# A decode layer's last weight columns spread unevenly over the DMA engines, and the last projection's tail cut anew

## The chip, the cores and the metric

One core of one Trainium2 chip runs the kernel. The metric is the device time of one execution in microseconds. Weights, cache and vectors lie in the chip's memory (DRAM) and are brought into the core's on-chip memory of 128 partitions by 16 DMA engines, which the issuing queues of SyncE (SP) and ScalarE (ACT) share. TensorE (PE) multiplies, VectorE (DVE), ScalarE and GpSimd (POOL) do the rest.

## The reference

One token of each of two sequences goes through a layer norm and then through attention over a cache and a gated linear unit in parallel; both results are added to x.

```python
W = min(4096, max(256, Sk // 4))                     # 4096 keys of 32768
xn = layernorm(x)                                    # [2, 1, 512]
q = (xn @ wq).reshape(B, 1, 32, 128)                 # 32 heads, 8 key heads
o = softmax(q @ k[-W:].T * 128 ** -0.5) @ v[-W:]
h = (xn @ W_gate) * (xn @ W_gate > 0) * (xn @ W_up)  # [2, 1, 1792]
out = x + o.reshape(B, 1, 4096) @ wo + h @ W_down
```

All is float32. The bytes are the 16 tiles of keys and values (4 MB each), wq and wo (8 MB each) and w_gate, w_up and w_down (3.5 MB each): 95 MB for two rows of x, so the work per byte is small.

## The kernel before, in words

**The ring.** All large operands go through one on-chip buffer, `ring` (L71), of four places of 8192 columns on 128 partitions. `place` hands the places out in turn: wq takes places 0 and 1, w_gate 2, w_up 3, then each tile of keys or values takes one, and at the end w_down and the two halves of wo. A place is loaded again when its last reader is done, which the issuing queue waits for. The first four tiles of the cache are two of keys (places 0 and 1, wq's) and two of values (place 2, w_gate's, and place 3, w_up's).

**Queues.** x (in three pieces, L121), all keys and values (L106), w_down (L95) and wo (L431) are issued by SyncE; wq, w_gate and w_up (L81) by ScalarE at the start, one behind the other, each as 128 rows, one to a partition. A transfer of 128 rows is divided among the 16 DMA engines, eight rows each.

**Order of the work.** The order on each engine is the order of the program. After the layer norm (L187 to L204) PE transposes xn (L208), VectorE copies it out 16 times over (xnT, L210), and PE multiplies with wq (L220). Then follow the products with w_gate and w_up (L257): x is the stationary operand of 32 columns, and the 1792 columns of the weight are cut into four quarters of 448 that go to four quarters of the PE array, so that four products run side by side. Row p of the on-chip tile holds the four rows 4p to 4p+3 of the weight, so there are four steps `kc`. VectorE forms h (hh, L266) and turns it (L270). Only behind that stand the first keys.

Then come four groups of one cache half and one sequence. In each, VectorE transposes two tiles of keys in halves (kT, L285), PE forms the scores (L291), a softmax follows (L306 to L327), and PE multiplies with two tiles of values (L348).

**The end.** y is summed in two ways. `slot` (L409) multiplies 128 rows of a weight by the stationary operand in one of four quarters of the PE array, taken in turn, over all 512 columns, into y4. Once `EARLY` of these are through, VectorE copies y4 to `ys` (L440), and four products with `fold` sum the quarters into y_ps. The rows of wo that are left go straight into y_ps as four products of 128 columns each (`quarters`, L416). ScalarE copies y_ps out (L444) and issues the store (L445). In words: w_down has 14 steps, each half of wo 16 rows (`j`); 8 steps of w_down go first, then the first half of wo, which comes in two transfers of eight rows, then 6 steps of w_down, then rows 0 to 7 of the second half as slots and rows 8 to 15 as quarters. The second half comes in four transfers (rows 0 to 7, 8 to 12, 13 and 14, 15).

Of the kernel before, what the change touches and what calls it, by code (L numbers as in the profile page):

```python
# [9 lines left out]
F32 = mybir.dt.float32  # L10
# [10 lines left out]
def kernel(  # L21
# [12 lines left out]
    nc = tc.nc  # L34
    P = 128
    B, _, D = x.shape
# [3 lines left out]
    F = w_gate.shape[1]  # L40
    W = min(4096, max(256, SK // 4))
    KC = D // P
# [3 lines left out]
    Q = 4  # L46
    C = 4
    R = HKV // C
# [14 lines left out]
    work = ctx.enter_context(tc.tile_pool(name="work", bufs=2))  # L63
    ps_kt = ctx.enter_context(tc.tile_pool(name="ps_kt", bufs=2, space=PSUM))
    ps_s = ctx.enter_context(tc.tile_pool(name="ps_s", bufs=1, space=PSUM))
    ps_1 = ctx.enter_context(tc.tile_pool(name="ps_1", bufs=1, space=PSUM))
# [7 lines left out]
    def place(cols):  # L74
        lo = taken[0] % RING * RW
        taken[0] += -(-cols // RW)
        return ring[:, lo:lo + cols]

    def load_rows(w):
        t = place(KC * w.shape[1])  # L80
        nc.scalar.dma_start(t, w.rearrange("(p k) f -> p (k f)", p=P))  # L81
        return t.rearrange("p (k f) -> p k f", k=KC)
# [5 lines left out]

    FM = F // P
    MQ = P * FM // Q  # L90
    assert P * FM == F

    def load_down():
# [16 lines left out]
    NJ = HQ * DH // (R * P)  # L110
# [3 lines left out]
    def wo_rows(r, j0, j1):  # L114
        rows = NJ * P
        return wo[r * rows:(r + 1) * rows, :].rearrange("(p j) e -> p j e", p=P)[:, j0:j1, :]
# [3 lines left out]
    for c0, c1 in ((0, 256), (256, 384), (384, 512)):  # L120
        nc.sync.dma_start(x2[:, c0:c1], x[:, 0, c0:c1])  # L121
    wqt = load_rows(wq)

    ident = const.tile([P, P], F32, name="ident")
    make_identity(nc, ident)
# [12 lines left out]
    oT = const.tile([P, R, NJ, B, 16], F32, name="oT")  # L138
# [64 lines left out]
    xn = work.tile([B, D], F32, name="xn", tag="qs")  # L203
    nc.vector.tensor_scalar(xn, xc, rs2, None, op0=ALU.mult)  # L204

    xt_ps = ps_1.tile([P, KC, B], F32, name="xt_ps", tag="misc")
    for kc in range(KC):
        nc.tensor.transpose(xt_ps[:, kc], xn.rearrange("r (p k) -> r k p", k=KC)[:, kc], ident[0:B, 0:B])  # L208
    xnT = work.tile([P, KC, 32], F32, name="xnT", tag="on", bufs=1)
    nc.vector.tensor_copy(  # L210
        xnT.rearrange("p k (b s) -> p k b s", b=B), xt_ps[:, :, :, None].to_broadcast([P, KC, B, 16])
    )


# [1 line left out]
    for kc in range(KC):  # L216
        for r in range(R):
            for c in range(C):
# [2 lines left out]
                    q_ps[r][32 * c:32 * c + 32, :], xnT[:, kc, :], wqt[:, kc, n * 512:(n + 1) * 512],  # L221
                    start=(kc == 0), stop=(kc == KC - 1),
                )
    gw = load_rows(w_gate)
    uw = load_rows(w_up)
    qT = work.tile([P, R, B, C, REP], F32, name="qT", tag="qT", bufs=1)
    for r in range(R):
        qs = work.tile([P, 512], F32, name=f"qs{r}", tag="qs")
# [13 lines left out]
    for pb in range(PB):  # L242
        rows = slice(L * pb, L * pb + L)
        for a in range(NP):
            lo = 2 * a * 16 + pb * REP
# [5 lines left out]

    g_ps = ps_kt.tile([P, MQ], F32, name="g_ps", tag="kt")
    u_ps = ps_kt.tile([P, MQ], F32, name="u_ps", tag="kt")
    for h, dst, wt in ((0, g_ps, gw), (1, u_ps, uw)):
        for kc in range(KC):
            for c in range(Q):
                nc.tensor.matmul(  # L257
                    dst[32 * c:32 * c + 32, :], xnT[:, kc, :], wt[:, kc, c * MQ:(c + 1) * MQ],
                    start=(kc == 0), stop=(kc == KC - 1),
                )  # L260
    gs = work.tile([P, MQ], F32, name="gs", tag="qs")
    nc.scalar.copy(gs, g_ps)
    gr = work.tile([P, MQ], F32, name="gr", tag="qs")
    nc.vector.scalar_tensor_tensor(gr, gs, 0.0, gs, op0=ALU.is_gt, op1=ALU.mult)
# [135 lines left out]
    nc.tensor.matmul(y_ps, xsel.rearrange("p e b s -> p (e b s)"), xr, start=True, stop=False)  # L400

    y4 = ps_kt.tile([P, D], F32, name="y4", tag="kt")
    cuts = {0: (0, NJ // 2, NJ), 1: (0, 8, 13, 15, NJ)}
    EARLY = FM + NJ + cuts[1][1]
    done = [0]

    def slot(lhsT, w):
        t, i = done[0] % Q, done[0]
        nc.tensor.matmul(  # L409
            y4[32 * t:32 * t + 32, :], lhsT.rearrange("p b s -> p (b s)"), w, start=(i < Q), stop=(i >= EARLY - Q)  # L410
        )
        done[0] += 1

    def quarters(lhsT, w, stop):
        for e in range(Q):
            nc.tensor.matmul(  # L416
                y_ps[32 * e:32 * e + 17, :], lhsT, w[:, e * P:(e + 1) * P], start=False, stop=stop
            )
# [4 lines left out]
    def down(k0, k1):  # L423
        for k in range(k0, k1):
            slot(hT[:, k], dw[:, k])

    down(0, 2 * Q)
    for r in range(R):
        wt = place(NJ * D).rearrange("p (j e) -> p j e", j=NJ)
        for j0, j1 in zip(cuts[r], cuts[r][1:]):  # L430
            nc.sync.dma_start(wt[:, j0:j1], wo_rows(r, j0, j1))  # L431
        if r == R - 1:
            down(2 * Q, FM)
        for j in range(NJ):
            if (r, j) < (1, cuts[1][1]):
                slot(oT[:, r, j], wt[:, j])
                continue
            if j == cuts[1][1]:
                ys = work.tile([P, D], F32, name="ys", tag="qs")
                nc.vector.tensor_copy(ys, y4)  # L440
                quarters(fold[:, 0:17], ys, False)
            quarters(oT[:, r, j].rearrange("p b s -> p (b s)")[:, 0:17], wt[:, j], (r, j) == (R - 1, NJ - 1))
    yo = work.tile([P, P], F32, name="yo", tag="yo", bufs=1)
    nc.scalar.copy(yo, y_ps)  # L444
    nc.scalar.dma_start(out[:, 0, :].rearrange("b (e f) -> e b f", e=Q), yo[0:P:16, :])  # L445
# [28 lines left out]
```

## Time and profile before

| | |
|---|---|
| median of 3 runs | 229.83 us (229.8 to 229.96) |
| the profiled execution | 229.9 us |
| its span, first to last instruction | 228.0 us |
| PE, DVE, ACT, POOL busy | 67%, 44%, 3%, 3% of the span |
| bytes moved | 95.03 MB, 417 GB/s over the span |
| ScalarE's queue and SyncE's queue | 15.74 MB and 79.17 MB |

Times in the views are microseconds from the span's start. A line of the timeline gives start, length, engine, source line, operation, what is written from what, how many, and in brackets how long the engine was idle before it and what ended that. A line of the windows gives a stretch, the busy time of each engine in it, the granted clock of PE, the mean busy share of the 16 DMA engines and GB/s; a DMA row counts in the stretch where it starts. In the list of issues the last figure is the time from issue to landing. In the chain of waits a line gives start, length and what the time went to.

### The profile page before, as it was taken

The numbers are of one execution on the slowest core, as the hardware profiler recorded it, in microseconds if no ns is written. First come the engines' busy times: TensorE is split into PE (matmuls) and PEld (weight loads), VectorE is DVE, ScalarE is ACT, GpSimd is POOL, SyncE is SP. The second block draws the span as 40 slices with busy tenths as digits, with TensorE's granted clock in tenths as the row PEclk, the third lists the DMA queues.
The fourth block names the chain that finished last, engine by engine and source line by source line (L and its number), as shares of the span: only waits on it lengthen the run. The fifth ranks groups of instructions, "written<-read, shape, count | busy, mean of one in ns | idle before, by whom it ended". The sixth has DMA issues, their size and how long they took to land.

```text
span 228.0 us, 2005 instructions
## 1 busy us (share of the span) xinstructions
PE 153.7 (67%) x870; PEld 45.0 (20%) x870; DVE 100.0 (44%) x89; ACT 6.8 (3%) x16; POOL 6.1 (3%) x21
## 2 busy tenths in 40 slices
PE   0010977036397668998668968858899885889764
PEld 0000223011121132331122212213131221222212
DVE  2040013003999223999421499922169972213000
ACT  0010012000000010000010000010000001000000
POOL 8100000000000000000000000000000000000000
PEclk9999999857589979999979999985799999599999
DMA  9898999999999999999999999999999999999991
GB/s 368 368 437 379 458 434 439 426 448 408 431 454 420 414 457 420 408 460 435 414 431 454 408 425 457 402 431 454 420 420 445 443 414 431 433 410 425 428 401 59
DMA packets 3792, 95.03 MB, mean 417 GB/s; under 512 B 434, under 2 KB 456, under 8 KB 712
## 3 DMA queue, kind: packets, MB, share of 16 engines
q1 hardware_dynamic: 3324, 79.17, 80.9%
q10 hardware_dynamic: 460, 15.74, 16.3%
q8 instruction: 7, 0.11, 0.2%
q14 instruction: 1, 0.01, 0.0%
HBM read 94.90 MB, written 0.00 MB: 416 GB/s over the span
## 4 chain that ended last, share of the span: by engine, by line
DMA 67%; DVE 14%; PE 9%; issue 8%; ACTq 1%; ACT 0%; DVEq 0%
DMA ring<-in_A_k_cache_dram 37%; DMA ring<-in_B_W_up_dram 21%; DVE kT L285 12%; DMA ring<-in_A_wo_dram 8%; PE u_ps L257 2%; PE s L291 2%; PE o L348 2%; PE pp L333 1%; PE y_ps L416 1%; PE y L409 1%; DVE pt L335 1%; DVE hh L266 0%; ACTq L81 0%; DVE ys L440 0%; DVE m L306 0%
## 5 line engine op out<-in xcount | busy, mean ns | idle before, releaser
L285 DVE STREAM_TRANSPOSE kT<-ring 128x4096 f32<-128x4096 f32 x16 | 70.0, 4417 | 7.0 <-DMA ring<-in_A_k_cache_dram 7.0
L291 PE MATMUL s<-kT,qz 128*32 128x512 f32 x256 | 58.3, 616 | 13.9 <-DVE kT L285 13.9
L348 PE MATMUL o<-ring,pt 128*32 128x512 f32 x256 | 33.0, 661 | 4.5 <-DVE rl L339 4.5
L291 PEld LDWEIGHTS s<-kT,qz 128*32 128x32 f32 x256 | 13.6, 109 | 57.7 <-issue 38.8
L333 PE MATMUL pp<-p,perm 128*128 128x512 f32 x16 | 13.4, 990 | 4.5 <-ACT p L327 4.5
L357 DVE TENSOR_TENSOR on<-o,mask 128x512 f32<-128x512 f32 x8 | 5.4, 676 | 23.6 <-PE o L348 23.6
L348 PEld LDWEIGHTS o<-ring,pt 128*32 128x32 f32 x256 | 8.1, 120 | 25.5 <-issue 20.7
L220 PE MATMUL q_ps<-ring,xnT 128*32 128x512 f32 x64 | 8.8, 710 | 5.9 <-DMA ring<-in_A_wq_dram 5.9
L257 PE MATMUL u_ps<-ring,xnT 128*32 128x448 f32 x32 | 5.3, 828 | 11.0 <-DMA ring<-in_B_W_up_dram 11.0
L335 DVE STREAM_TRANSPOSE pt<-pp 128x1024 f32<-128x1024 f32 x4 | 5.0, 1250 | 17.2 <-PE pp L333 17.2
L208 PE MATMUL xt_ps<-ident,xn 2*128 2x2 f32 x4 | 0.6, 252 | 16.4 <-DVE xn L204 16.4
L363 PE MATMUL oa<-on,picks 128*128 128x512 f32 x16 | 9.0, 645 | 3.7 <-DVE on L357 3.7
L409 PE MATMUL y<-ring,oT 128*32 128x512 f32 x48 | 5.7, 596 | 2.9 <-DMA ring<-in_A_wo_dram 2.9
L306 DVE TENSOR_REDUCE m<-s 128x1 f32<-128x512 f32 x4 | 2.8, 692 | 11.1 <-PE s L291 11.1
L266 DVE TENSOR_TENSOR hh<-gr,u_ps 128x448 f32<-128x448 f32 x1 | 0.9, 908 | 15.0 <-PE u_ps L257 15.0
L235 DVE COPY qT<-qt 128x32 f32<-128x32 f32 x2 | 0.4, 192 | 15.8 <-PE qt L232 15.8
L327 ACT ACTIVATE p<-s,nm 128x512 f32<-128x512 f32 x4 | 2.7, 687 | 150.3 <-DVE nm L321 150.3
L299 PE MATMUL idle<-pt,ident 128*128 128x512 f32 x12 | 6.0, 618 | 0.0
L333 PEld LDWEIGHTS pp<-p,perm 128*128 128x128 f32 x16 | 3.8, 261 | 8.2 <-issue 4.6
L440 DVE COPY ys<-y 128x512 f32<-128x512 f32 x1 | 0.7, 692 | 10.7 <-PE y L409 10.7
L187 DVE BATCH_NORM_STATS2 stats<-x 2x6 f32<-2x512 f32 x1 | 0.7, 682 | 10.6 <-DMA x<-in_A_x_dram 10.6
L220 PEld LDWEIGHTS q_ps<-ring,xnT 128*32 128x32 f32 x64 | 2.4, 128 | 11.4 <-issue 11.4
(72 smaller groups left out, 59.8 us busy)
## 6 DMA issues: line engine op xcount, KB each, us to landing
ring<-in_A_k_cache_dram SPq DMA_DIRECT2D x8, 4096.0 KB, 28.5
ring<-in_A_v_cache_dram SPq DMA_DIRECT2D x8, 4096.0 KB, 24.2
ring<-in_A_wo_dram SPq DMA_DIRECT2D x3, 2048.0 KB, 28.5
ring<-in_B_W_gate_dram ACTq DMA_DIRECT2D x1, 3584.0 KB, 30.1
ring<-in_B_W_up_dram ACTq DMA_DIRECT2D x1, 3584.0 KB
ring<-in_B_W_down_dram SPq DMA_DIRECT2D x1, 3584.0 KB, 29.0
ring<-in_A_wo_dram SPq DMA_DIRECT2D x1, 1280.0 KB
ring<-in_A_wo_dram SPq DMA_DIRECT2D x1, 512.0 KB, 21.4
```

Of the source, the lines that this page charges most:

```text
L220: nc.tensor.matmul(q_ps[r][32 * c:32 * c + 32, :], xnT[:, kc, :], wqt[:, kc, n * 512:(n + 1) * 512], start=(kc == 0), stop=(kc == KC - 1),)
L257: nc.tensor.matmul(dst[32 * c:32 * c + 32, :], xnT[:, kc, :], wt[:, kc, c * MQ:(c + 1) * MQ], start=(kc == 0), stop=(kc == KC - 1),)
L285: nc.vector.transpose(kt.rearrange("p j c k h -> p (j c k h)"), kt_in[:, JH * s1 * DH:JH * (s1 + 1) * DH])
L291: nc.tensor.matmul(ss[g][lo:lo + 32, :], qz[:, g, cb, h, 16 * a:16 * a + 32], kt[:, :, cb, :, h], start=(a == 0 and cb == 0), stop=(a == N ...
L299: nc.tensor.matmul(idle, ident, pts[g][:, 2 * n:2 * n + 2].rearrange("p n j k -> p (n j k)"), start=True, stop=True)
L306: nc.vector.tensor_reduce(out=m, in_=ss[g], op=ALU.max, axis=AX.X)
L333: nc.tensor.matmul(pp[:, h], perm[:, h], p, start=True, stop=True)
L335: nc.vector.transpose(pts[g].rearrange("p n j k -> p j n k"), pp.rearrange("p h y -> p y h"))
L348: nc.tensor.matmul(o[32 * q:32 * q + 32, :], pts[g][:, a * S1 + s1, j:j + 4, :].rearrange("p u k -> p (u k)"), v[:, lo:lo + 512], start=(s ...
L357: nc.vector.tensor_tensor(ons[a], os[a].rearrange("p (u d) -> p u d", u=4), mask[:, :, None].to_broadcast([P, 4, P]), op=ALU.mult)
L363: nc.tensor.matmul(oa[g].rearrange("p u e j -> p u (e j)"), picks[:, a].rearrange("p h a i e -> p (h a i e)"), ons[a], start=(a == 0), sto ...
L409: nc.tensor.matmul(y4[32 * t:32 * t + 32, :], lhsT.rearrange("p b s -> p (b s)"), w, start=(i < Q), stop=(i >= EARLY - Q))
```

## The change

**w_up.** Its place is loaded with all but the last 320 columns of the last of the four rows on each partition (`UC`: 6848 of 7168 columns). Those 128 pieces of 320 columns (1280 bytes) go elsewhere: into four strips of 320 columns behind, which are set to zero first. `SMALL` lists four transfers: two of 20 pieces over five engines into strip 0 (four pieces each), and two of 36 pieces over three engines into strips 1 to 3 (twelve each); a fifth brings the last 16 pieces over 16 engines. All five stand behind w_up's main part on ScalarE's queue. A piece's partition is then no longer that of its row of x, so the last of the four parts of xn is laid out again for each strip (`xe`, by GpSimd), transposed by PE into four further columns of xnT, and multiplied with the strips in four further products of 320 columns on the last quarter of the array, behind the other products of w_up; the product that they replace is cut from 448 to 128 columns.

**The issue of w_gate and w_up** is written earlier in the program; on ScalarE's queue it stays where it was, behind wq's.

**wo and w_down.** The first half of wo comes in one transfer. The six last steps of w_down go ahead of it instead of behind it. Of the second half ten rows, not eight, are slots; its transfers are rows 0 to 9, 10 to 12, 13 and 14, and two half rows of row 15.

```diff
@@ -88,6 +88,14 @@
 
     FM = F // P
     MQ = P * FM // Q
+    MX = 320
+    ES = 4
+    SMALL = []
+    at = 0
+    for e, s0, s1 in ((5, 0, 1), (3, 1, ES)):
+        for h in range(2):
+            SMALL.append((e, h, s0, s1, at))
+            at += 4 * e * (s1 - s0)
     assert P * FM == F
 
     def load_down():
@@ -120,6 +128,20 @@
     for c0, c1 in ((0, 256), (256, 384), (384, 512)):
         nc.sync.dma_start(x2[:, c0:c1], x[:, 0, c0:c1])
     wqt = load_rows(wq)
+    gw = load_rows(w_gate)
+    UC = KC * F - MX
+    ut = place(UC + ES * MX)
+    nc.vector.memset(ut[:, UC:], 0.0)
+    nc.scalar.dma_start(ut[:, :UC], w_up.rearrange("(p k) f -> p (k f)", p=P)[:, :UC])
+    apart = w_up.rearrange("(p k) f -> p (k f)", p=P)[:, UC:]
+    for e, h, s0, s1, p0 in SMALL:
+        src = bass.AP(
+            tensor=apart.tensor, offset=apart[p0:p0 + 1].offset,
+            ap=[[KC * F, e], [KC * F * e, 4 * (s1 - s0)], [1, MX]],
+        )
+        nc.scalar.dma_start(ut[32 * h:32 * h + 4 * e, UC + s0 * MX:UC + s1 * MX], src)
+    nc.scalar.dma_start(ut[64:64 + P - at, UC:UC + MX], apart[at:P])
+    uw = ut[:, :KC * F].rearrange("p (k f) -> p k f", k=KC)
 
     ident = const.tile([P, P], F32, name="ident")
     make_identity(nc, ident)
@@ -203,12 +225,23 @@
     xn = work.tile([B, D], F32, name="xn", tag="qs")
     nc.vector.tensor_scalar(xn, xc, rs2, None, op0=ALU.mult)
 
-    xt_ps = ps_1.tile([P, KC, B], F32, name="xt_ps", tag="misc")
+    xt_ps = ps_1.tile([P, KC + ES, B], F32, name="xt_ps", tag="misc")
     for kc in range(KC):
         nc.tensor.transpose(xt_ps[:, kc], xn.rearrange("r (p k) -> r k p", k=KC)[:, kc], ident[0:B, 0:B])
-    xnT = work.tile([P, KC, 32], F32, name="xnT", tag="on", bufs=1)
+    last = xn.rearrange("r (p k) -> r k p", k=KC)[:, KC - 1]
+    xe = work.tile([B, ES, P], F32, name="xe", tag="qs")
+    nc.gpsimd.memset(xe, 0.0)
+    for e, h, s0, s1, p0 in SMALL:
+        nc.gpsimd.tensor_copy(
+            xe[:, s0:s1, 32 * h:32 * h + 4 * e].rearrange("r s (e t) -> r s e t", t=4),
+            last[:, p0:p0 + 4 * e * (s1 - s0)].rearrange("r (t s e) -> r s e t", t=4, e=e),
+        )
+    nc.gpsimd.tensor_copy(xe[:, 0, 64:64 + P - at], last[:, at:P])
+    for s in range(ES):
+        nc.tensor.transpose(xt_ps[:, KC + s], xe[:, s], ident[0:B, 0:B])
+    xnT = work.tile([P, KC + ES, 32], F32, name="xnT", tag="on", bufs=1)
     nc.vector.tensor_copy(
-        xnT.rearrange("p k (b s) -> p k b s", b=B), xt_ps[:, :, :, None].to_broadcast([P, KC, B, 16])
+        xnT.rearrange("p k (b s) -> p k b s", b=B), xt_ps[:, :, :, None].to_broadcast([P, KC + ES, B, 16])
     )
 
 
@@ -221,8 +254,6 @@
                     q_ps[r][32 * c:32 * c + 32, :], xnT[:, kc, :], wqt[:, kc, n * 512:(n + 1) * 512],
                     start=(kc == 0), stop=(kc == KC - 1),
                 )
-    gw = load_rows(w_gate)
-    uw = load_rows(w_up)
     qT = work.tile([P, R, B, C, REP], F32, name="qT", tag="qT", bufs=1)
     for r in range(R):
         qs = work.tile([P, 512], F32, name=f"qs{r}", tag="qs")
@@ -254,10 +285,16 @@
     for h, dst, wt in ((0, g_ps, gw), (1, u_ps, uw)):
         for kc in range(KC):
             for c in range(Q):
+                w = MQ - MX if (h, kc, c) == (1, KC - 1, Q - 1) else MQ
                 nc.tensor.matmul(
-                    dst[32 * c:32 * c + 32, :], xnT[:, kc, :], wt[:, kc, c * MQ:(c + 1) * MQ],
-                    start=(kc == 0), stop=(kc == KC - 1),
+                    dst[32 * c:32 * c + 32, 0:w], xnT[:, kc, :], wt[:, kc, c * MQ:c * MQ + w],
+                    start=(kc == 0), stop=(kc == KC - 1 and w == MQ),
                 )
+    for s in range(ES):
+        nc.tensor.matmul(
+            u_ps[32 * Q - 32:32 * Q, MQ - MX:], xnT[:, KC + s, :], ut[:, UC + s * MX:UC + (s + 1) * MX],
+            start=False, stop=(s == ES - 1),
+        )
     gs = work.tile([P, MQ], F32, name="gs", tag="qs")
     nc.scalar.copy(gs, g_ps)
     gr = work.tile([P, MQ], F32, name="gr", tag="qs")
@@ -400,8 +437,9 @@
     nc.tensor.matmul(y_ps, xsel.rearrange("p e b s -> p (e b s)"), xr, start=True, stop=False)
 
     y4 = ps_kt.tile([P, D], F32, name="y4", tag="kt")
-    cuts = {0: (0, NJ // 2, NJ), 1: (0, 8, 13, 15, NJ)}
-    EARLY = FM + NJ + cuts[1][1]
+    LATE = 10
+    cuts = {0: (0, NJ), 1: (0, LATE, 13, 15, NJ - 0.5, NJ)}
+    EARLY = FM + NJ + LATE
     done = [0]
 
     def slot(lhsT, w):
@@ -426,20 +464,22 @@
 
     down(0, 2 * Q)
     for r in range(R):
-        wt = place(NJ * D).rearrange("p (j e) -> p j e", j=NJ)
-        for j0, j1 in zip(cuts[r], cuts[r][1:]):
-            nc.sync.dma_start(wt[:, j0:j1], wo_rows(r, j0, j1))
-        if r == R - 1:
+        flat = place(NJ * D)
+        wt = flat.rearrange("p (j e) -> p j e", j=NJ)
+        rows = wo_rows(r, 0, NJ).rearrange("p j e -> p (j e)")
+        for lo, hi in zip(cuts[r], cuts[r][1:]):
+            nc.sync.dma_start(flat[:, int(lo * D):int(hi * D)], rows[:, int(lo * D):int(hi * D)])
+        if r == 0:
             down(2 * Q, FM)
         for j in range(NJ):
-            if (r, j) < (1, cuts[1][1]):
+            if r == 0 or j < LATE:
                 slot(oT[:, r, j], wt[:, j])
                 continue
-            if j == cuts[1][1]:
+            if j == LATE:
                 ys = work.tile([P, D], F32, name="ys", tag="qs")
                 nc.vector.tensor_copy(ys, y4)
                 quarters(fold[:, 0:17], ys, False)
-            quarters(oT[:, r, j].rearrange("p b s -> p (b s)")[:, 0:17], wt[:, j], (r, j) == (R - 1, NJ - 1))
+            quarters(oT[:, r, j].rearrange("p b s -> p (b s)")[:, 0:17], wt[:, j], j == NJ - 1)
     yo = work.tile([P, P], F32, name="yo", tag="yo", bufs=1)
     nc.scalar.copy(yo, y_ps)
     nc.scalar.dma_start(out[:, 0, :].rearrange("b (e f) -> e b f", e=Q), yo[0:P:16, :])
```

## The prediction

> **What bounds the kernel now.** I read the page first, then the DMA windows at the end, the chain of waits, SyncE's issues, and the end of the timeline.
>
> ```profile
> span 228.0 us, 2005 instructions
> DMA  9898999999999999999999999999999999999991
> q8 instruction: 7, 0.11, 0.2%
> DMA 67%; DVE 14%; PE 9%; issue 8%; ACTq 1%; ACT 0%; DVEq 0%
> ```
>
> The 16 DMA engines are busy from the first slice to the last but one, and two thirds of the chain is DMA. Who moves the end must shorten the slowest DMA engine's list, or what follows its last byte. The seven instruction packets took 0.2% of 16 x 228 us, so about 1.0 us each, and each sits on one engine, which stays late from then on, as nothing idles. The end shows the spread:
>
> ```profile
> 222.00:223.00 1.00, 0.41 (x16) 0.34 (x20) 0.53 (x1) 0.00 (x0) 0.00 (x0) 1.00 0.76 299
> 223.00:224.00 1.00, 1.00 (x41) 0.81 (x32) 0.00 (x0) 0.00 (x0) 0.00 (x0) 1.00 0.35 135
> 224.00:225.00 1.00, 1.00 (x28) 0.48 (x24) 0.00 (x0) 0.00 (x0) 0.00 (x0) 1.00 0.07 20
> ```
>
> In the last column but one the DMA share falls: 0.76, 0.35, 0.07. The mean engine ends near 222 + 1.18 = 223.2, and between 223 and 224 some six of 16 are still at it. That imbalance is what moving rows can win.
>
> **The bytes (a gain).** Each engine carries 8 of 128 rows of w_up. By the lists in the diff 112 rows' last 1280 B go elsewhere: engines 0 to 2 carry 8 + 24 + 1 = 33 such pieces, 3 and 4 carry 9, the other eleven 1. Prices:
>
> ```profile
> ring<-in_A_wq_dram ACTq DMA_DIRECT2D x1, 22.0
> ring<-in_B_W_gate_dram ACTq DMA_DIRECT2D x1, 3584.0 KB, 30.1
> 0.74 0.39 ACTq L81 DMA_DIRECT2D ring<-in_A_wq_dram  x1
> 1.17 0.44 ACTq L81 DMA_DIRECT2D ring<-in_B_W_gate_dram  x1
> 202.55 0.42 SPq L431 DMA_DIRECT2D ring<-in_A_wo_dram  x1
> 203.07 0.38 SPq L431 DMA_DIRECT2D ring<-in_A_wo_dram  x1
> ring<-in_A_wo_dram SPq DMA_DIRECT2D x1, 256.0 KB, 21.5
> ring<-in_A_wo_dram SPq DMA_DIRECT2D x1, 512.0 KB, 21.4
> ```
>
> wq lands at 22.7 and w_gate at 31.3: 8.5 us for 8 rows of 28 KB on each engine, 1.06 us a row, 0.047 us per 1280 B. So eleven engines, the late ones I take to be among them, lose 7 x 0.047 = 0.33 us. wo's last row (the 256 KB) lands at 203.07 + 21.5 = 224.6 and the 512 KB before it at 202.55 + 21.4 = 223.95, so 8 pieces of 2 KB take 0.63 us, 0.08 us each at most for a piece of 1280 B. Engines 0 to 2 gain 33 x (0.05 to 0.08) - 0.38 = 1.3 to 2.3 us; I take 1.3, as 1280 B lie nearer to the proportional price. That fits under the spread of 1.4 us between mean and last, barely. If a late engine is among 0 to 2, the end comes 1.0 us later instead.
>
> **When the small pieces arrive (the loss I expect).** They stand on ACT's queue behind wq, w_gate and w_up's main part, and SyncE's queue has K and V beside them. How do two queues share an engine?
>
> ```profile
> 0.74 0.95 SPq L121 DMA_DIRECT2D x<-in_A_x_dram  x3
> 13.04 0.68 DVE L187 BATCH_NORM_STATS2 stats<-x 2x6 f32<-2x512 f32 x1 [10.57 <-DMA x<-in_A_x_dram]
> 35.25 3.21 PE L257 MATMUL g_ps<-ring,xnT 128*32 128x448 f32 x32
> 49.47 5.28 PE L257 MATMUL u_ps<-ring,xnT 128*32 128x448 f32 x32 [11.01 <-DMA ring<-in_B_W_up_dram]
> ```
>
> x is 4 KB in three transfers issued by 1.7 us, yet its reader starts at 13.04: wq's rows of 64 KB take some (22.0 - 1.0) / 8 = 2.6 us each, and the second and third x transfer, a piece and a completion each, took about four turns of that. w_up tells the same: 8.5 us alone, it lands 18.1 us after w_gate, as 8 K rows (9.7 us, below) go turn about with its own. So one piece passes per turn, however small, and the other queue's whole row goes between.
>
> The Trainium skill, "DMA: Bandwidth & Descriptors", section "Queues, rings and completion order", says otherwise: an engine drains a packet of typically 9 to 17 descriptors from one queue before it turns to the next. By that the pieces would pass in three or four turns and the sum would be that of the first rival. The trace of x and w_up does not agree with it, their parts went one by one; many small parts of one transfer it does not hold.
>
> ```profile
> 99.13 0.04 DVE kT L285
> 176.85 0.04 DVE kT L285
> 38.52 0.53 SPq L106 DMA_DIRECT2D ring<-in_A_v_cache_dram  x1
> ring<-in_A_v_cache_dram SPq DMA_DIRECT2D x1, 4096.0 KB, 31.5
> 54.80 0.54 SPq L106 DMA_DIRECT2D ring<-in_A_v_cache_dram  x1
> 65.08 0.54 SPq L106 DMA_DIRECT2D ring<-in_A_k_cache_dram  x1
> 89.00 0.53 SPq L106 DMA_DIRECT2D ring<-in_A_v_cache_dram  x1
> 123.40 6.05 SPq L106 DMA_DIRECT2D ring<-in_A_v_cache_dram  x2
> 1.00:2.00 1.00, 0.00 (x0) 0.00 (x0) 0.66 (x3) 0.00 (x0) 0.98 (x2) 1.00 2.23 723
> 2.00:3.00 1.00, 0.00 (x0) 0.00 (x0) 0.47 (x2) 0.00 (x0) 1.00 (x2) 1.00 0.90 328
> ```
>
> Two groups of four tiles take 176.85 - 99.13 = 77.7 us: 9.7 us a tile, 1.21 us for a K row of 32 KB. Engines 0 to 2 have 33 pieces and 5 completions, 38 x 1.21 = 46 us if K and V last that long. They do not: the second V tile goes into w_up's own place in the ring, and today SyncE issues it at 54.80, just as u_ps ends (49.47 + 5.28). Until u_ps is done the queue holds three tiles only; the first V lands at 38.52 + 31.5 = 70.0. Then the rest of the pieces, some 15 to 20, run alone at 0.05 to 0.08 us. So the last piece lands near 70.2.
>
> Behind it PE has three of the four new products, of two passes each, all on one quarter of the array and so one after another: u_ps's 32 took 5.28 us, four at a time after the idle stretch, so 0.66 us a pass of 448 columns and 0.47 of 320. Six are 2.8 us (1.7 at g_ps's rate). u_ps ends at about 73.3, 18.5 us later than now. VectorE has hh and then the K transposes in order behind it, PE the scores, and SyncE the second V tile.
>
> Stall one: V is issued at 73.3 and moves about 1.0 us later (of the first rows of 64 KB, issued at 0.74, the windows start 0.72 MB or 11 in the second microsecond and 5 in the third); the mean engine ran dry 1.4 us ahead of the last landing, less the 0.33: 68.3. That is 6.0 us. The next K needs the transposes of the first: today 10.3 us after u_ps, so 83.6 + 1.0, while V ends at 84.0: 0.6 us. The next V needs the first V consumed: 34.2 us after u_ps, 107.5 + 1.0, while two K tiles end at 104.0: 4.5 us. Later tiles keep ahead, since a group of compute takes at most 34.4 us (the same V issue comes at 89.00 and 123.40) against 4 x 9.7 = 38.9 of DMA. Sum 11.1 us. If three pieces went in a turn and PE ran at g_ps's rate, u_ps would end at 70.4 and 8.2 us were left; if the pieces landed before 60, nothing, and a gain has no source, since no byte is saved. From above, 13.5 us, with the pieces late by two more K rows. I take 11.1, from the nearest rows.
>
> **The end (a smaller loss).** One transfer now brings ten rows of wo to the plain products, not eight, and six follow in quarters.
>
> ```profile
> 214.79 1.92 PE L409 MATMUL y<-ring,oT 128*32 128x512 f32 x16 [1.55 <-DMA ring<-in_A_wo_dram]
> 216.53 1.89 PE L409 MATMUL y<-ring,hT 128*32 128x512 f32 x12
> 219.65 0.14 issue
> 219.79 1.92 PE L409 MATMUL y<-ring,oT 128*32 128x512 f32 x16 [1.37 <-DMA ring<-in_A_wo_dram]
> 221.84 0.69 DVE L440 COPY ys<-y 128x512 f32<-128x512 f32 x1 [10.65 <-PE y L409]
> 222.59 0.41 PE L416 MATMUL y_ps<-ys,fold 128*17 128x128 f32 x8 [0.87 <-DVE ys L440]
> 222.79 1.02 PEld L416 LDWEIGHTS y_ps<-ring,oT 128*17 128x17 f32 x40
> 224.66 0.13 PEld L416 LDWEIGHTS y_ps<-ring,oT 128*17 128x17 f32 x8 [0.28 <-DMA ring<-in_A_wo_dram]
> 225.15 0.27 ACT yo L444
> ```
>
> Ten rows land 6 x 0.63 us before the last: 220.8, or 220.5 with the 0.33; the eight landed at 219.65. Eight products take 1.92 us, but six take 1.89: they go by fours, 0.87 us a four (216.53 - 214.79 for two). Ten are three fours: 2.8 us. Today ys's fold starts 2.80 us after PE starts at 219.79; then it starts 3.67 us after 220.64, at 224.3. Then 0.2 us of fold, five rows at 0.2 us (40 loads in 1.02) and 0.49 us for the last row up to ACT's copy (224.66 to 225.15): 226.1 against 225.15, so 0.95 us later. The half rows gain nothing, since PE no longer waits for them; where it did, they would save one of two batches, 0.1 us.
>
> **What costs nothing.** x once more: five small copies and a memset on GpSimd and four transposes.
>
> ```profile
> L180 POOL COPY perm<-ident 128x32 f32<-128x32 f32 x4 | 0.7, 209 | 0.1
> 22.91 8.77 PE L220 MATMUL q_ps<-ring,xnT 128*32 128x512 f32 x64 [5.92 <-DMA ring<-in_A_wq_dram]
> ```
>
> Six POOL instructions at some 0.2 us are 1.3 us, the transposes half a microsecond, under PE's 5.92 us of waiting for wq. The memset of the ring's tail runs in VectorE's idle 10.57 us, and ACT's five extra issues (0.44 us each) before it has other work. Moving six products of w_down ahead of wo's first half fills a wait on its DMA. PE's instructions: 24 more early, 24 fewer at the end, so instruction packets stay as many; one more would cost an engine 1.0 us.
>
> **The sum.** The profiled execution took 229.9 us (span 228.0), the median is 229.83. 229.9 + 11.1 + 0.95 = 241.95: **242.0 us**. Own range 238 (8.2 us, less what lining up the engines gives back) to 245.5 (13.5 us, and engines 0 to 2 late by 1.0 at the end).
>
> **Rivals.**
> 1. The small pieces come at once: drained several to a turn, they need some four turns of 1.3 us behind w_up's landing at 49.4 and land by 55; u_ps ends near 57, and no V starves (it has until 68). Left is the end: 229.9 + 0.95 = **230.9**. For it: nobody has seen many small pieces of one transfer share an engine here. Against: x's and w_up's turns. This is the skill's packet rule at work.
> 2. The end is set by the slowest DMA engine, not by PE: pieces come early and the ten products, copy and six rows fit the 3.8 us between the ten rows' landing and the last. Then 0.33 us fewer on the late engines and 0.1 from the half row: **229.5**, faster by 0.2%. It decides where the chain from the ten rows to ACT's copy takes under 225.15 - 220.5 = 4.6 us; the rows give 5.6.
> 3. It does not do what it says: the pieces spread over all engines, no balance, no long queue; the end as in 1 without the 0.33: **231.2**.
>
> **How the numbers follow.** My case 0.62, rival 1 0.18, rival 3 0.03, something between (a stall of a few microseconds) 0.04, rival 2 0.13. The range takes in my case and rivals 1 and 3: 230.7 to 245.5. A measurement tells 0.2% (0.46 us) from no change; rival 2 lies near that line, so faster 0.09, same 0.05, slower 0.86.
>
> **What would show it.** DMA slices with gaps near 70 and 105 us; PE's wait before the new products for w_up of over 10 us; SyncE's second V issue past 70; at the end no PE wait on the last three wo transfers. If u_ps ends before 60, my turns are wrong; if PE still waits for the last half row, my end is wrong.

## The result and the profile after

The kernel after takes 245.11 us (median of 6 runs, 243.33 to 246.04) against 229.88 us (6 runs, 229.8 to 230.17): a ratio of 1.0647, 95% interval 1.06 to 1.0693. It is slower by 15.2 us; the forecast was 12.2 us. The profiled execution took 245.75 us, 15.85 us more than the one of before, and its span is 244.0 us.

The page first: the span, the DMA row in 40 slices of 6.1 us, GB/s in the same slices, and the shares of the chain.

```profile
span 244.0 us, 2018 instructions
DMA  9799999999906999948999999999999999999980
GB/s 344 344 516 393 399 442 438 451 434 417 433 33 258 430 365 419 419 175 344 426 427 430 430 430 430 427 430 430 430 430 430 443 435 430 430 431 435 419 342 14
q8 instruction: 7, 0.11, 0.2%
DMA 49%; DVE 21%; PE 18%; issue 10%; ACT 1%; ACTq 0%; DVEq 0%
```

The row of nines has two holes: slices 11 and 12, counted from 0 (67 to 79 us; 33 and 258 GB/s), and slice 17 (104 to 110 us; 175 GB/s). DMA fell from 67% of the chain to 49%; that share alone tells little, as run 4 below, which has no such hole, stands at 47%. What the chain holds around the first hole tells more:

```profile
31.26 38.91 DMA ring<-in_B_W_up_dram
70.17 0.14 issue
70.30 4.01 PE u_ps L294 x8
74.31 0.02 issue
74.33 0.92 DVE hh L303
```

The last piece of w_up lands at 70.17. All four new products (eight passes) follow it, and only then hh and the keys. SyncE's issues that hang on this, each from its own stretch of the timeline, are the second V tile, the K tile behind it and the V tile after those:

```profile
74.33 0.53 SPq L114 DMA_DIRECT2D ring<-in_A_v_cache_dram  x1
84.60 0.54 SPq L114 DMA_DIRECT2D ring<-in_A_k_cache_dram  x1
109.73 0.54 SPq L114 DMA_DIRECT2D ring<-in_A_v_cache_dram  x1
```

The windows tell what the holes cost. First the kernel after, then the kernel before in the same stretches; the last figure is GB/s.

```profile
66.00:76.00 10.00, 4.00 (x8) 1.24 (x8) 1.63 (x3) 0.00 (x0) 0.00 (x0) 0.61 0.31 112
76.00:104.00 28.00, 18.88 (x72) 5.51 (x72) 19.66 (x10) 0.78 (x2) 0.00 (x0) 0.82 0.98 410
104.00:112.00 8.00, 6.89 (x39) 1.69 (x43) 2.54 (x4) 0.00 (x0) 0.00 (x0) 0.76 0.45 158
```

```profile
66.00:76.00 10.00, 8.70 (x43) 2.00 (x40) 7.70 (x2) 0.00 (x0) 0.00 (x0) 1.00 0.98 423
76.00:104.00 28.00, 22.97 (x122) 7.02 (x120) 17.53 (x13) 0.78 (x2) 0.00 (x0) 0.94 1.00 430
104.00:112.00 8.00, 7.04 (x32) 1.53 (x28) 5.48 (x5) 0.00 (x0) 0.00 (x0) 1.00 1.05 445
```

Bytes missing, at 430 GB/s: 10 x (423 - 112) is 3.11 MB or 7.2 us; 28 x (430 - 410) is 0.56 MB or 1.3 us; 8 x (445 - 158) is 2.30 MB or 5.3 us. Together 13.9 us.

The end, by the chain. A transfer of wo lands, 20 passes, the copy, the fold and the quarters, ScalarE's copy:

```profile
214.81 20.49 DMA ring<-in_A_wo_dram
235.43 2.78 PE y L447 x20
238.31 0.70 DVE ys L480
239.05 1.77 PE y_ps L454 x56
```

```profile
240.84 0.27 ACT L484 COPY yo<-y_ps 128x128 f32<-128x128 f32 x1 [33.73 <-PE y_ps L454]
```

From the landing (214.81 + 20.49 = 235.30) to ScalarE's copy at 240.84 there is no wait for a DMA: 5.54 us. The copy stood at 225.15 before, so 15.69 of the 15.85 us are made ahead of it.

### The profile page after: what moved, and what is told of

Its sections match the earlier page's. It is cut to its first block, busy times and chain, and to the rows that moved or that the text cites. A ratio compares the mean times of both kernels' runs of the same rounds, so it can differ in the third digit from the quotient of the medians.

```text
span 244.0 us, 2018 instructions
## 1 busy us (share of the span) xinstructions
PE 157.5 (65%) x870; PEld 47.6 (20%) x870; DVE 100.9 (41%) x90; ACT 6.8 (3%) x16; POOL 7.5 (3%) x27
## 2 busy tenths in 40 slices
DMA packets 3952, 95.03 MB, mean 390 GB/s; under 512 B 466, under 2 KB 872, under 8 KB 1128
## 4 chain that ended last, share of the span: by engine, by line
DMA 49%; DVE 21%; PE 18%; issue 10%; ACT 1%; ACTq 0%; DVEq 0%
DVE kT L322 16%; DMA ring<-in_B_W_up_dram 16%; DMA ring<-in_B_W_gate_dram 12%; DMA ring<-in_A_k_cache_dram 12%; DMA ring<-in_A_wo_dram 8%; PE o L385 5%; PE s L328 5%; PE pp L370 4%; PE u_ps L294 2%; DVE pt L372 2%; PE y L447 1%; DVE on L394 1%; DVE m L343 1%; ACT p L364 1%; PE y_ps L454 1%
## 5 line engine op out<-in xcount | busy, mean ns | idle before, releaser
L328 PE MATMUL s<-kT,qz 128*32 128x512 f32 x256 | 56.7, 619 | 11.5 <-DVE kT L322 11.3
L385 PE MATMUL o<-ring,pt 128*32 128x512 f32 x256 | 30.9, 625 | 4.8 <-DVE rl L376 4.8
L294 PE MATMUL u_ps<-ring,xnT 128*32 128x320 f32 x8 | 4.0, 676 | 15.8 <-DMA ring<-in_B_W_up_dram 15.8
L447 PE MATMUL y<-ring,oT 128*32 128x512 f32 x52 | 6.4, 595 | 5.1 <-DMA ring<-in_A_wo_dram 5.1
L289 PE MATMUL u_ps<-ring,xnT 128*32 128x448 f32 (+1 forms) x32 | 5.1, 788 | 5.7 <-DMA ring<-in_B_W_up_dram 5.7
L370 PEld LDWEIGHTS pp<-p,perm 128*128 128x128 f32 x16 | 4.3, 299 | 8.4 <-ACT p L364 4.8
L289 PE MATMUL g_ps<-ring,xnT 128*32 128x448 f32 x32 | 5.6, 877 | 0.0
```

The costliest lines, as they stand in the source:

```text
L289: nc.tensor.matmul(dst[32 * c:32 * c + 32, 0:w], xnT[:, kc, :], wt[:, kc, c * MQ:c * MQ + w], start=(kc == 0), stop=(kc == KC - 1 and w == ...
L294: nc.tensor.matmul(u_ps[32 * Q - 32:32 * Q, MQ - MX:], xnT[:, KC + s, :], ut[:, UC + s * MX:UC + (s + 1) * MX], start=False, stop=(s == ES ...
L328: nc.tensor.matmul(ss[g][lo:lo + 32, :], qz[:, g, cb, h, 16 * a:16 * a + 32], kt[:, :, cb, :, h], start=(a == 0 and cb == 0), stop=(a == N ...
L370: nc.tensor.matmul(pp[:, h], perm[:, h], p, start=True, stop=True)
L385: nc.tensor.matmul(o[32 * q:32 * q + 32, :], pts[g][:, a * S1 + s1, j:j + 4, :].rearrange("p u k -> p (u k)"), v[:, lo:lo + 512], start=(s ...
L447: nc.tensor.matmul(y4[32 * t:32 * t + 32, :], lhsT.rearrange("p b s -> p (b s)"), w, start=(i < Q), stop=(i >= EARLY - Q))
```

## The experiments

**Theory:** small pieces pass one per turn beside K and V rows; the late u_ps starves the ring; the new end adds about 1.2 us. **Rivals:** the uneven spread or x's new layout makes the loss, the pieces drain several to a turn, or the end is DMA's. In the runs, "before" is the kernel before on the same chip, 229.84 to 229.93 us.

**1. The new end alone** (the kernel before, with the diff's last two hunks).

> The kernel before with the changed end alone: first half of wo in one transfer, six steps of w_down ahead of it, ten rows as slots, the last row in halves; w_up is loaded as before. My theory (PE's chain from the ten rows to ACT's copy takes 5.6 us and sets the end): ten rows land at 220.9, ACT copies at 226.4 instead of 225.15, so 231.1 to 231.2 us, and PE waits for none of the last three wo transfers. Rival (the end is set by the last landing): 229.8, with a wait for the last half row.

Measured: 231.93 us, ratio 1.0096 [1.0068, 1.0125]. The six runs lie in two groups, 231.05 to 231.15 and 232.7 to 233.02; the profiled one is of the lower. Its chain at the end:

```profile
220.84 0.14 issue
220.97 2.78 PE y L410 x20
223.85 0.70 DVE ys L443
224.60 1.77 PE y_ps L417 x56
226.39 0.27 ACT yo L447
```

The ten rows land at 220.84, and 5.55 us of passes and copies follow without a DMA wait. The copy comes 1.24 us later than before. TensorE's side sets this end, and the DMA rival falls. The lower group is where the theory put the time; the median isn't, and what makes the upper group, 1.6 us more, this run doesn't show (see run 9).

**2. The pieces alone** (the change with the end of before).

```diff
-    LATE = 10
-    cuts = {0: (0, NJ), 1: (0, LATE, 13, 15, NJ - 0.5, NJ)}
-    EARLY = FM + NJ + LATE
+    cuts = {0: (0, NJ // 2, NJ), 1: (0, 8, 13, 15, NJ)}
+    EARLY = FM + NJ + cuts[1][1]
...
-        if r == 0:
+        if r == R - 1:
             down(2 * Q, FM)
```

> The changed kernel with the end of before: the uneven pieces alone. My theory (one piece per turn, a whole K or V row between): the new products start at 70 again, two gaps in the DMA, about 244 us, 1.2 under the changed kernel. Rival (the large loss comes from the new order at the end as well, or from both together): 232 to 240.

Measured: 244.98 us, ratio 1.0666 [1.0638, 1.0694]. TensorE's wait for the pieces, from the timeline:

```profile
70.44 4.44 PE L294 MATMUL u_ps<-ring,xnT 128*32 128x320 f32 x8 [17.39 <-DMA ring<-in_B_W_up_dram]
```

The pieces alone make a loss as large as the whole change's. The new end's 1.2 us isn't to be seen in the difference from the kernel after (244.98 against 245.11). The runs of either spread over 2 to 3 us, and in this run's profile the later V tile is issued at 111.55, 1.8 us behind the 109.73 of the kernel after, so this pair can't weigh the end.

**3. The pieces ahead of w_gate and of w_up's main part.**

```diff
-    gw = load_rows(w_gate)
     UC = KC * F - MX
+    gt = place(KC * F)
...
-    nc.scalar.dma_start(ut[:, :UC], w_up.rearrange("(p k) f -> p (k f)", p=P)[:, :UC])
...
     nc.scalar.dma_start(ut[64:64 + P - at, UC:UC + MX], apart[at:P])
+    nc.scalar.dma_start(gt, w_gate.rearrange("(p k) f -> p (k f)", p=P))
+    gw = gt.rearrange("p (k f) -> p k f", k=KC)
+    nc.scalar.dma_start(ut[:, :UC], w_up.rearrange("(p k) f -> p (k f)", p=P)[:, :UC])
```

> The changed kernel with the five transfers of pieces issued ahead of w_gate and w_up's main part, so that no K or V is beside them. My theory: they run alone behind wq, three engines lose some 1.3 us there, PE's new products follow the others at once near 55, no gap in the DMA; left is the new end, 230.7 to 231.3 us. Rival (three engines cannot carry these pieces, or the extra products and x's second layout hold PE): gaps stay, over 235.

Measured: 235.05 us, ratio 1.0221 [1.0195, 1.0247]. Ten of the 15 us are gone, and the holes near 70 and 105 with them, yet not the four more that were expected. ScalarE's queue and two windows say why:

```profile
22.78 0.35 ACTq L142 DMA_DIRECT2D ring<-in_B_W_up_dram  x1
23.17 0.43 ACTq L143 DMA_DIRECT2D ring<-in_B_W_gate_dram  x1
```

```profile
20.00:24.00 4.00, 1.11 (x8) 0.46 (x12) 0.00 (x0) 0.00 (x0) 0.00 (x0) 1.00 0.14 40
10.00:40.00 30.00, 15.87 (x96) 7.03 (x100) 4.06 (x14) 2.38 (x4) 1.94 (x7) 0.93 0.91 377
```

The fifth small transfer is issued only at 22.78, when wq has landed, and w_gate stands behind it: from 20 to 24 us the DMA engines move 40 GB/s (265 before). From 10 to 40 us it is 377 GB/s against 421 before, 1.3 MB or 3.1 us, most of the four. The chain of this run names wq's transfer as the releaser.

**4. As many pieces, evenly** (the kernel before; w_up in a main part and one transfer of the last 320 columns; eight pieces and a completion on each engine; no layout of x, no new products).

```diff
-    uw = load_rows(w_up)
+    nc.scalar.dma_start(ut[:, :UC], rows[:, :UC])
+    nc.scalar.dma_start(ut[:, UC:], rows[:, UC:])
```

> The kernel before with w_up loaded in two transfers, the main part and the last 320 columns of each row as a second one over all 16 engines: 8 pieces and a completion on each engine, at the same place of the queue. My theory: nine turns of 1.22 us behind w_up's 47.4, so PE's last product of w_up waits until 58 to 60, u_ps ends near 60, the second V still comes in time (before 68): time as before, 229.7 to 230.3. Rival (several pieces drained to a turn): the wait ends by 51.

**5. The same, twice** (the last 320 columns in two transfers of 160: 16 pieces and two completions on each engine).

```diff
+    for c0 in (UC, UC + 160):
+        nc.scalar.dma_start(ut[:, c0:c0 + 160], rows[:, c0:c0 + 160])
```

> The kernel before with w_up in three transfers over all 16 engines: the main part and the last 320 columns in two of 160, so 16 pieces and two completions on each engine, 18 turns. No uneven spread, no second layout of x, no new products. My theory: the pieces last as long as K and V do, PE's last product waits to 68 or 69, the second V is issued near 70, a first gap of some 3 us and one of 5 us at the next V, 235 to 239 us. Rival (the uneven spread over three engines, or x's second layout, makes the loss): time as with 8 pieces, 230.6.

Measured: 230.63 us, ratio 1.0018 [1.0008, 1.0029], for one transfer, and 238.41 us, ratio 1.0396 [1.0361, 1.0431], for two. With one transfer the wait ends where the theory put it, but the time is 0.3 us above its range (the nine runs lie at 229.82 to 230.06 and at 230.63 to 230.77); what costs it is not shown. The last two passes of u_ps, first with one transfer, then with two:

```profile
58.94 1.70 PE L262 MATMUL u_ps<-ring,xnT 128*32 128x448 f32 x2 [4.58 <-DMA ring<-in_B_W_up_dram]
```

```profile
69.07 1.67 PE L263 MATMUL u_ps<-ring,xnT 128*32 128x448 f32 x2 [14.45 <-DMA ring<-in_B_W_up_dram]
```

Nine more turns on each engine put the end of w_up off by 69.07 - 58.94 = 10.1 us, 1.1 us a turn, with no byte more: close to the 1.21 us of a K row. The windows of the second:

```profile
66.00:76.00 10.00, 1.67 (x2) 0.18 (x2) 5.19 (x3) 0.00 (x0) 0.00 (x0) 0.50 0.55 216
76.00:104.00 28.00, 21.55 (x104) 5.77 (x104) 16.79 (x12) 0.78 (x2) 0.00 (x0) 0.91 0.95 394
104.00:112.00 8.00, 7.65 (x44) 2.28 (x46) 8.00 (x3) 0.00 (x0) 0.00 (x0) 1.00 0.97 385
```

Against the same rows of before, 2.07, 1.01 and 0.48 MB are missing, 8.3 us at 430 GB/s; the kernel is 8.6 us slower. So the number of turns alone makes such a loss, without an uneven spread, a layout of x or new products. (The sum was forecast better than its parts: the first gap is 4.8 us instead of 3, what follows 3.5 instead of 5.) Pieces that drain several to a turn fall too: the Trainium skill's 9 to 17 descriptors ("DMA: Bandwidth & Descriptors", section "Queues, rings and completion order") would have let nine parts pass in one turn or two; at 1.1 us for each of the nine more they took a turn each here, and the measurement decides.

**6. The pieces first, and x in one transfer instead of three.**

> As the run with the pieces first, with x in one transfer instead of three, so that w_gate need not wait for a free semaphore at 23 us. My theory (the 3 us that the run with the pieces first lost beyond the new end are DMA time lost between 21.6 and 24.7, where w_gate was issued only when wq had landed): no gap there, the new end alone is left, 230.7 to 231.5 us. Rival (three engines with more pieces or the new products cost by themselves): 233 or more.

Measured: 232.62 us (231.28 to 234.63), ratio 1.0135 [1.009, 1.0181]. w_gate is now issued at 6.50 and the hole at 20 to 24 us is no deeper than before (255 GB/s); run 8 shows that x's transfers by themselves are worth nothing, so the 2.4 us from run 3 to this one go to the freed queue. It is still slower than the kernel before by more than the new end's 1.24 us accounts for, and so outside the theory's range, short of the rival's 233. In its profile TensorE starts on the ten rows at 221.99, behind their landing, 1.0 us later than in run 1 (220.97), and from there to ScalarE's copy it takes as long (5.41 and 5.42 us). So the rest is lost ahead of that landing; where, is open.

**7. The same with the end of before**, so with the balance of rows as the only aim left.

> The same with the end of before. My theory: the even lists at last, with PE's chain at the end as before: 229.5 us if the seventh instruction packet still comes behind the last bytes, 230.5 if PE's 24 more instructions bring it in front of them. Rival (the balance gives nothing, other engines are the late ones): 229.9 to 231.

**8. The control: the kernel before with x in one transfer.**

```diff
-    for c0, c1 in ((0, 256), (256, 384), (384, 512)):
-        nc.sync.dma_start(x2[:, c0:c1], x[:, 0, c0:c1])
+    nc.sync.dma_start(x2, x[:, 0, :])
```

> The kernel before with x in one transfer instead of three, the control for the kernels with the pieces first and x in one. Theory: x is read long before wq lands at 22.7, so nothing moves, 229.7 to 229.95 us. Rival: the two or four turns fewer on the first engines let wq and all behind it land up to 0.3 us earlier, 229.5 us.

Measured: 230.10 us (229.89 to 232.63), ratio 1.0022 [1.0003, 1.0041], for run 7, and 230.07 us, ratio 1.0005 [0.9996, 1.0014], for the control. The balance wins nothing that can be measured, as run 7's rival had it. Its profile shows where it fails. The windows at the end:

```profile
222.00:223.00 1.00, 0.14 (x7) 0.13 (x8) 0.69 (x1) 0.00 (x0) 0.00 (x0) 1.00 0.78 313
223.00:224.00 1.00, 1.00 (x44) 0.97 (x41) 0.00 (x0) 0.00 (x0) 0.00 (x0) 1.00 0.53 207
224.00:225.00 1.00, 1.00 (x36) 0.55 (x28) 0.00 (x0) 0.00 (x0) 0.00 (x0) 1.00 0.08 27
```

The shares 0.78, 0.53 and 0.08 put the mean engine's end at 222 + 1.39 = 223.4, no earlier than the 223.2 of before, and a few engines still run past 224. TensorE has a slow stretch ahead of the end: it waits 2.97 us for wo and then takes 3.53 us for sixteen passes that took 1.92 before.

```profile
215.05 3.53 PE L447 MATMUL y<-ring,oT 128*32 128x512 f32 x16 [2.97 <-DMA ring<-in_A_wo_dram]
```

It catches up, though. The last weight load (PEld), that of wo's last row, waits for the DMA again:

```profile
224.90 0.13 PEld L454 LDWEIGHTS y_ps<-ring,oT 128*17 128x17 f32 x8 [0.28 <-DMA ring<-in_A_wo_dram]
```

Before, this load stood at 224.66 with the same 0.28 us of waiting. So the last row lands 0.24 us later, not 0.33 us earlier, and ScalarE's copy follows by 0.23 us (225.38 against 225.15). The slowest DMA engine's list sets this end too, and it was not shortened: the last landing is some 1.5 us behind the mean engine's end, 1.4 before.

**9. Run 7 with six steps of w_down moved ahead of wo's first half**, as the change does it, to fill that wait.

```diff
-        if r == R - 1:
+        if r == 0:
             down(2 * Q, FM)
```

> The pieces first, x in one transfer and the end of before, with the change's early six steps of w_down. In the profile of the kernel without that last part, TensorE waited 2.97 us for wo until 215.05, took 3.53 us for sixteen passes that take 1.92 us at full clock, and from there worked through to ScalarE's copy at 225.38 without a wait for the last rows. Theory (TensorE's slow start at the end hides what the balance of the rows wins): with twelve passes moved ahead of the wait TensorE is done before the last row lands, the last row 0.33 us earlier than in the kernel before, ScalarE's copy at 224.8, 229.5 us. Rival (the slowest DMA engine is not among those that were relieved): the last row lands as before, copy at 225.1 to 225.4, 229.8 to 230.1 us.

Measured: 231.27 us (229.98 to 233.38), ratio 1.0066 [1.004, 1.0092]. Neither expectation held, and the premise "without a wait for the last rows" was a misreading of run 7, as its last load shows. The profiled execution is a long one, 232.42 us. Its last plain products, and a window with the granted clock behind ScalarE's, VectorE's and GpSimd's columns:

```profile
221.24 3.20 PE L447 MATMUL y<-ring,oT 128*32 128x512 f32 x16 [3.07 <-DMA ring<-in_A_wo_dram]
```

```profile
223.00:225.00 2.00, 1.44 (x8) 0.00 (x0) 0.44 (x1) 0.00 (x0) 0.00 (x0) 0.50 0.36 141
```

With w_down out of the way TensorE waits 3.07 us for the next rows of wo, and the clock falls to 0.50 right where every product counts: 3.20 us for sixteen passes, 1.3 us more than before. Moving w_down ahead didn't shorten the waiting for wo's larger transfers (0.92 and 2.97 us in run 7, 0.82 and 3.07 us here), it put the longer wait nearer to the end. The half clock is only a part of the copy's delay here (227.53 against 225.15): the rows that TensorE waits for, issued at 200.53, land at 221.11 instead of 219.65, 1.5 us later, and why is not shown. The upper group of run 1, whose order of the end is the same, would fit a half clock over its last passes, but no run of it was profiled; that is argued, not shown.

**10. The half rows alone** (the kernel before, wo's last row in two transfers).

```diff
-    cuts = {0: (0, NJ // 2, NJ), 1: (0, 8, 13, 15, NJ)}
+    cuts = {0: (0, NJ // 2, NJ), 1: (0, 8, 13, 15, NJ - 0.5, NJ)}
```

> The kernel before with wo's last row in two half rows, nothing else. My theory: PE's last wait is for the last half row, behind which stand two products and not four: 0.1 us less, 229.8. Rival (one more transfer and completion costs as much as it saves): 229.9 to 230.0.

Measured: 229.83 us, ratio 0.9998 [0.9989, 1.0006]; ScalarE's copy stands at 225.06 instead of 225.15. No gain that a measurement can tell.

No version was faster than the kernel before.

## Why the prediction was right, and which terms were mis-sized

**The landing at 70.2** was right (70.17), and so was its reason. Runs 4 and 5 give 1.1 us a turn; at that pace the 38 turns of engines 0 to 2 would have lasted past 90 us, so they ended when K and V ran out. For the same reason the landing doesn't test the pace: any list of more than about 19 turns ((70.0 - 49.4) / 1.1) would have lasted until then. What shows the pace is runs 4 and 5.

**The new products** were mis-sized. "Three of the four", six passes in 2.8 us, were to follow the landing; it was all four, eight passes in 4.00 us:

```profile
70.30 4.00 PE L294 MATMUL u_ps<-ring,xnT 128*32 128x320 f32 x8 [15.83 <-DMA ring<-in_B_W_up_dram]
```

```profile
70.00:72.00 2.00, 1.70 (x4) 0.66 (x5) 0.00 (x0) 0.00 (x0) 0.00 (x0) 0.50 0.00 0
72.00:74.00 2.00, 2.00 (x6) 0.58 (x4) 0.00 (x0) 0.00 (x0) 0.00 (x0) 0.57 0.00 0
```

The first strip was overlooked: the fifth transfer writes into it too, and its pieces stand last in the long lists of engines 0 to 2. The price of a pass (0.50 against 0.47) was near. So u_ps ended at 74.3, not 73.3, and the first stall was 7.2 us, not 6.0.

**The K issue** came 1.0 us late with it, 84.60 for 83.6; the stretch to 104 lost 1.3 us, not 0.6.

**The V issue** at 109.73 (forecast 107.5) stands 35.4 us behind u_ps's end, not 34.2, and the third stall was 5.3 us, not 4.5. The products with the values, first after, then before:

```profile
104.28 5.38 PE L385 MATMUL o<-ring,pt 128*32 128x512 f32 x32 [1.12 <-DVE rl L376]
```

```profile
85.30 3.64 PE L348 MATMUL o<-ring,pt 128*32 128x512 f32 x32 [1.12 <-DVE rl L339]
```

They took 1.7 us longer. TensorE's clock, 0.68 around these products (104 to 110 us) and 0.97 around those of before (84 to 90 us), was not part of the forecast's 34.2 us. The later tiles kept ahead, as forecast.

**The end** was forecast at 1.28 us for the ten rows less 0.33 us for the balance. Run 1 gives 1.24 us and 5.55 us from landing to copy (forecast 5.6): right, though the prediction's own rows add up to 226.0, not 226.1. The 0.33 us failed: in run 7 the last row lands 0.24 us later, where the prediction took the last engines to be relieved. Whether they weren't among the eleven, or the pieces cost all engines more than was counted, is open, as the profile doesn't tell one DMA engine from another. Stalls of 15.69 - 1.24 = 14.45 us (13.9 by the three windows) and this end make the profiled 15.7; the forecast had 11.1 and 0.95.

**What was to cost nothing** cost nothing: TensorE still waits 4.67 us for wq, where it waited 5.92. One thing wasn't foreseen, ScalarE's late issues:

```profile
22.81 3.74 ACTq L142 DMA_DIRECT2D ring<-in_B_W_up_dram  x4
31.26 0.35 ACTq L143 DMA_DIRECT2D ring<-in_B_W_up_dram  x1
33.01 0.59 ACT L260 COPY qs<-q_ps 128x512 f32<-128x512 f32 x1
```

The small transfers weren't issued "before it has other work" but at 22.81 and 31.26, and the copy of q behind them starts at 33.01 instead of 30.88. The 2.1 us lay under the wait for the pieces; in run 3 the same kind of wait was on the path.

**The rivals.** Pieces drained several to a turn: out by runs 4 and 5. An end set by DMA: out by run 1. A change that doesn't do what it says: the kernel after has 3952 DMA packets where the kernel before has 3792, and the 160 more are 128 pieces and 32 completions, as many as the lists' 5 + 5 + 3 + 3 + 16 engines (run 4's one transfer more makes 144: 128 pieces and 16 completions). So the pieces went over as many engines as the lists say; run 7, which keeps those lists and takes the stalls away, shows no gain from them.

## What to carry to other kernels

Count the turns, not the bytes, of a transfer that shares DMA engines with a queue of long rows: each small part waited for a whole row of the other queue, so a balance by small pieces belongs where the other queue is empty, or nothing may hang on its landing. Before moving rows to win a fraction of a microsecond, follow who gives the next buffer free: here one late product held the ring's place and cost 14 us. Work that is moved out of the way of a wait can move the idle time, and TensorE may run its next passes at half clock, as in run 9.

## What the runs showed of the hardware that was not expected

- TensorE was granted half clock after waits of 2.97 and 3.07 us (3.53 and 3.20 us for sixteen passes, 1.92 at full clock) and full clock after one of 2.57 us (20 passes in 2.78 us). The Trainium skill, "TensorE: Matmul & The Clock Gate", section "What's actually happening", lets the clock fall after an idle window of about 3.4 us; here shorter waits were enough. In run 9 the clock fell only when the passes were under way again (1.00 from 221.0 to 221.5 us, 0.50 from 222 to 223), so the length of the wait alone doesn't decide.
- An issuing queue can wait by itself: five small transfers behind three large ones left ScalarE's issue standing until wq had landed (22.81), and the last until w_gate had (31.26); in run 4 a single one stood until 22.68. With x in one transfer and the pieces first, all issues were out by 7.4 us (run 6). That completion counters are reused and must come free first is a possible reason, argued only.
